# A planned attention and gate kernel: planning in forward and backward rounds, and another order of the first loads

## The chip, the cores and the metric

The kernel runs on one core of a Trainium2 chip. The metric is the device time in microseconds (us), as the median of several executions; one execution of each kernel is also taken with the hardware profiler. A core has five engines that run on their own and meet at semaphores: TensorE (PE, matrix products and transposes; its weight loads are shown apart as PEld), VectorE (DVE), ScalarE (ACT), GpSimd (POOL) and SyncE (SP). Loads and stores are DMAs, which SP, ACT and POOL issue. Here POOL's loads can also turn fp32 in memory into fp16 on the way.

## What is computed

Inputs are q, k, v of 8 batches x 8 heads x 576 positions x 64 columns, 32 packed queries p for each head, and three matrices. All are fp32, and so is the output of 8 x 576 x 512.

```python
def sm_attn(qq, kk, vv):
    a = softmax(qq @ kk.T / 8)
    return a @ vv
packed = sm_attn(p, k, v)               # 32 rows for each head
x = sm_attn(q, packed, packed)          # heads side by side: 576 x 512 a batch
proj = x @ w_proj                       # 512 -> 3 * 512
x1, x2, x3 = thirds of proj
x2_conv = irfft(rfft(x2, axis=seq) * rfft(filter, axis=seq))
out = (x1 * x2_conv * x3) @ w_out
```

The Fourier transforms are real ones along the 576 positions; here they are matrix products with cosine and sine tables.

## The kernel before

**Stages.** Each batch goes through four generators. `front(b)` (line 536) turns the keys on TensorE (`k_turn`), makes scores with the packed queries (`score1`, and `e1` by Exp), multiplies with the values (`pv`), turns the queries (`q_turn`, tile `qT`), and makes the second attention's weights (`score2` to `e2`; `normal` on DVE and POOL gives `a2n` and the tail). `turn(b)` (692) projects the 32 packed rows of each head with `w_proj` (`project`, tile `qm`), and takes the spectrum of the attention weights (`fp`, `fa`) and their transpose (`a2t`). So the attention's output is never formed: its product with each matrix is taken through the packed rows. `middle(b)` (754) makes the products with the spectrum of x2 (`f`, DVE's products with the filter `tt`, POOL's sums `gm`) and the two gates (`x1`, `x3`, kept as `w`). `back(b)` (809) does the inverse transform (products of `gm` and the table `ac`), multiplies with `w` to `y`, projects with `w_out` (`o`) and stores. `prologue_filter` (501) does the filter's spectrum once, in two fp16 halves (`fh`, `fl`, products into `hp`, results in `h3` and `htail`).

**Staggering.** `together` (883) interleaves the generators by the costs that they yield. In round b of the loop at line 911, `front(b)`, `turn(b-1)`, `middle(b-2)` and `back(b-3)` run together, with exceptions at the start.

**The planner.** Nothing is issued at once: a `Recorder` (line 145) keeps each instruction as an `Op`. `depend` (180) finds what must come before what, `plan` (205) plays the program with a price for each operation (`Op.ns`, `product`, `transfer_ns`) and the limits on buffers, and `emit` (369) issues in that order, each engine's order fixed. All instructions thus carry line 373 in the profile, and are told apart by tile names. The rule that orders ready operations on an engine is one line, `choose` (292): the first in the order in which the program recorded them. A load from POOL needs one of eight lanes, free again when it lands. Where PE has nothing ready, `filler` (266) puts in a product on zeros (`spin`), between 4.5 and 34 us of the plan and while a window of 3.4 us has less than 3.5 us of work.

**First loads.** From line 475 on: SP loads `ident`, the filter (six DMAs) and `ac`; ACT loads the tables `wc` (four) and `wt`; POOL loads p and q's tail of batch 0 (`load_small`), keys, values and queries of batch 0, three parts of `w_proj`, then batch 1 and `w_out`. `load(b)` for later batches is called two rounds ahead; from batch 4 on, SP turns the queries by a transposing DMA.

Of the kernel before, what the change touches and what calls it, by code (L numbers as in the profile page):

```python
# [17 lines left out]
P = 128  # L18
# [65 lines left out]
class Op:  # L84


    def __init__(self, n, engine, call, what, args, kw):
        self.n, self.engine, self.call, self.what, self.args, self.kw = n, engine, call, what, args, kw
        named = dict(kw)
        rest = [a for a in args if isinstance(a, bass.AP)]  # L90
        self.out = named.pop("out") if "out" in named else rest.pop(0)
        self.ins = rest + [a for a in named.values() if isinstance(a, bass.AP)]
        self.writes = [r for r in map(region, [self.out]) if r]
        self.reads = [r for r in map(region, self.ins) if r]
        size = lambda x: x.size() // x.shape[0]
        self.columns = size(self.out) if engine == "PE" else max(map(size, [self.out] + self.ins[:1]))
        self.need, self.then, self.unit = 0, [], None
        self.mode, self.place = (128, 128), None
        if engine == "PE":

            k, m = self.ins[0].shape[0], self.out.shape[0]
            self.mode = (64 if k <= 64 else 128), (m + 31) // 32 * 32
            self.place = self.reads[0][1] // self.mode[0], self.writes[0][1] // self.mode[1]

    def ns(self):
# [14 lines left out]
    def transfer_ns(self):  # L120
# [4 lines left out]
        if self.what == "dma_start_transpose":  # L125
            piece, size, self.piece_ns = 256, self.out.size() * 2, 22
        return size / piece * self.piece_ns / 16


# [12 lines left out]
class Recorder:  # L142
# [37 lines left out]
    def depend(self):  # L180

        seen, self.users, bank = {}, {}, {}
        for op in self.ops:
# [13 lines left out]
            if op.engine == "PE":  # L197

                before |= {bank[t] for t, *_ in op.writes if t in bank}
                bank.update({t: op for t, *_ in op.writes})  # L200
            op.need = len(before)
            for o in before:
                o.then.append(op)

    def plan(self):

        self.depend()
        opened = set()
        limit = {tag: bufs for kinds in self.slot.values() for tag, bufs in kinds}
# [56 lines left out]
        def filler(t):  # L266

            if 4500 < t < self.keep_warm and busy.get(int(t // window), 0) < warm + 300 and used["ps"] < limit["ps"]:
                op = self.spin()
# [7 lines left out]
        def fits(op, held):  # L277
# [7 lines left out]
            if any(used[tag] + held.get(tag, 0) + n > limit[tag] for tag, n in more.items()):  # L285
# [3 lines left out]
                return False  # L289
            return op.what[:9] != "dma_start" or op.engine != "POOL" or lanes[0] > 0  # L290

        def choose(e):
            held = {}
            return next((o for o in sorted(ready[e], key=lambda o: o.n) if fits(o, held)), None)

        def release(op, same):
            for o in op.then:
                if (o.engine == op.engine and op.what[:9] != "dma_start") == same:
                    o.need -= 1
# [3 lines left out]
        def issue(e, t):  # L303
            while free[e] <= t + 1e-6:
# [16 lines left out]
                order.append(op)  # L321
                if op.what[:9] == "dma_start":
                    took = 760 if e == "POOL" else 60
# [16 lines left out]
        while events:  # L340
            t, _, what, x = heapq.heappop(events)
            if what == "done":
                release(x, False)
# [22 lines left out]
        assert sum(op.n < 10 ** 9 for op in order) == len(self.ops), "the plan stops short"  # L366
        return order

# [11 lines left out]
def kernel(  # L380
# [56 lines left out]
    qTms = [const.tile([P, 2, 2, P], FP16, tag=f"qTm{r}", name=f"qTm{r}") for r in range(2)]  # L437
    filt = [sb([P, DM], FP32, tag="os", name=f"filt{i}", bufs=5) for i in range(5)]

# [7 lines left out]
    def load_small(b, n):  # L447

        pn = const.tile([P, n, 2, D], FP16, tag=f"pn{b}", name=f"pn_b{b}")
        qt = const.tile([P, n, H // 2, D], FP16, tag=f"qt{b}", name=f"qt_b{b}")  # L450
        nc.gpsimd.dma_start(pn[:], pflat[:, b:b + n, :, :])
        tail = q[b:b + n, :, 512:576, :].rearrange("b (g u) s d -> u s b g d", u=2)
        for u in range(2):
            nc.gpsimd.dma_start(qt[u * 64:(u + 1) * 64, :, :, :], tail[u])
        for x in range(n):
            small[b + x] = pn[:, x, :, :], qt[:, x, :, :]

    def load(b):
# [4 lines left out]
        qn = sb([P, H, 4 * D], FP16, tag="qn", name=f"qn_b{b}")  # L463
        nc.gpsimd.dma_start(kn[:], k[b].rearrange("h (p i) d -> p h (i d)", i=KI))
        nc.gpsimd.dma_start(vn[:], v[b].rearrange("h (p i) d -> p h (i d)", i=KI))
        nc.gpsimd.dma_start(qn[:], q[b, :, 0:512, :].rearrange("h (p i) d -> p h (i d)", i=4))
        if b in (2, 4):
# [8 lines left out]
    nc.sync.dma_start(ident[:], d_id.ap()[:])  # L476
    for i in range(4):
        nc.scalar.dma_start(wc[:, i, :], d_wc.ap()[:, i, :])
        nc.sync.dma_start(filt[i][:], fsrc[:, TILE_I[i], :])
    nc.scalar.dma_start(wt[:], d_wt.ap()[:])  # L480
    nc.sync.dma_start(filt[4][0:32, :], ftail[0])
    nc.sync.dma_start(filt[4][32:64, :], ftail[1])
    load(0)
    wsrc = moe_w_proj.rearrange("(g r) c -> r g c", r=P)
    for c in (1, 0, 2):
        nc.gpsimd.dma_start(wp[:, :, ts(c, DM)], wsrc[:, :, ts(c, DM)])
    nc.sync.dma_start(ac[:], d_ac.ap()[:])
    load(1)
# [410 lines left out]
    h = prologue_filter()  # L899
    some(h, 3)  # L900
    together((h, 4000.0), (front(0), 5500.0))
    first = turn(0)
# [27 lines left out]

    nc.spin, nc.keep_warm = spin, 34000
    nc.emit()

# [29 lines left out]
```

## Time and profile before

| | us |
|---|---|
| median of 4 runs | 204.92 |
| lowest, highest | 203.04, 207.04 |
| the profiled execution's own time | 206.22 |
| its span, first to last instruction | 204.4 |

| engine | busy us | share of the span |
|---|---|---|
| PE | 189.1 | 93% |
| DVE | 142.4 | 70% |
| POOL | 133.4 | 65% |
| ACT | 125.8 | 62% |

Names with a buffer number stand without it (`kn_b` is the keys of any batch). A line of the chain of waits is a start, a duration and what ran or was waited for; a group or a load names output<-input, the engine, the operation, and the count. "To landing" is from the issue to the completion of a DMA. PE's busy time counts a product from issue to its last result, and products overlap, so it isn't its use of the array.

### The profile page before, as it was taken

To read this page: it belongs to the slowest core of one execution; us is meant where nothing else is said; L and a number is where in the kernel's file an instruction comes from. 1 tells how busy PE (TensorE), PEld (TensorE's weight loads), DVE (VectorE), ACT (ScalarE), POOL (GpSimd) and SP (SyncE) were. 2 spreads that over 40 slices of the span, in tenths; PEclk is the share of its full clock that TensorE was granted. 3 is DMA by queue.
4 is the path that set the end of the run, shared out by engine and by line. 5 is a ranking of instruction groups with operands and counts; after the bars stand their busy time and mean duration, and the time that the engine had idled before them with its cause. 6 is when DMAs were issued, how large, how long until landed. Compare 5 with 4: busy or idle time off the path is not lost.

```text
span 204.4 us, 5828 instructions
## 1 busy us (share of the span) xinstructions
PE 189.1 (93%) x2419; PEld 117.3 (57%) x2419; DVE 142.4 (70%) x268; ACT 125.8 (62%) x265; POOL 133.4 (65%) x108
## 2 busy tenths in 40 slices
PE   3989978999999998999899999999999999999990
PEld 2335755665765674765476656656665565664640
DVE  4331683999528789876868589768876897688610
ACT  3234575775688968658766777676767746415140
POOL 7712339839753979986986796489548993972200
PEclk9997699999999999999999999999999999999997
DMA  6999999999999999999999993124012202413335
GB/s 162 268 245 201 207 196 201 204 201 189 201 185 260 207 152 161 140 146 196 257 230 166 168 197 110 50 81 128 3 51 84 76 0 104 129 29 115 95 115 141
DMA packets 44843, 30.96 MB, mean 151 GB/s; under 512 B 16336, under 2 KB 39376, under 8 KB 44816
## 3 DMA queue, kind: packets, MB, share of 16 engines
q0 software_dynamic: 29312, 16.52, 59.8%
q1 hardware_dynamic: 14784, 13.34, 26.8%
q10 hardware_dynamic: 720, 0.72, 1.3%
q8 instruction: 19, 0.31, 0.6%
q14 instruction: 8, 0.07, 0.1%
HBM read 35.55 MB, written 9.44 MB: 220 GB/s over the span
## 4 chain that ended last, share of the span: by engine, by line
PE 68%; POOL 10%; DMA 10%; ACT 5%; issue 2%; DVE 1%; POOLq 0%; ACTq 0%; DVEq 0%
PE x_b L373 24%; PE o_b L373 13%; PE f_b L373 6%; DMA kn_b<-in_k_dram 6%; PE fp_b L373 5%; PE s_b L373 4%; DMA qT_b<-qn_b 4%; POOL gm_b L373 3%; PE pv_b L373 3%; PE kTp_b L373 3%; POOL fa_b L373 2%; POOL tt_b L373 2%; ACT qm_b L373 2%; PE qp_b L373 2%; PE qTp_b L373 2%
## 5 line engine op out<-in xcount | busy, mean ns | idle before, releaser
L373 POOL TENSOR_TENSOR gm_b<-tt_b,tt_b 128x512 f16<-128x512 f32 (+1 forms) x28 | 39.2, 1427 | 9.7 <-DVE tt_b L373 9.2
L373 PE MATMUL x_b<-a2t_b,qm_b 128*128 128x512 f16 (+1 forms) x256 | 40.9, 286 | 0.0
L373 DVE TENSOR_TENSOR tt_b<-f_b,h 128x1024 f32<-128x1024 f32 x32 | 39.1, 1220 | 2.1 <-POOL gm_b L373 0.9
L373 PE MATMUL x_b<-ac,gm_b 128*128 128x64 f16 (+3 forms) x312 | 35.9, 253 | 2.0 <-POOL gm_b L373 1.7
L373 ACT ACTIVATE os_b<-o_b 128x512 f32<-128x512 f32 x36 | 21.6, 599 | 22.5 <-PE o_b L373 22.1
L373 PE MATMUL o_b<-wout,y_b 128*128 128x512 f16 x128 | 33.0, 379 | 0.1
L373 ACT CAST qm_b<-qp_b 128x512 f16<-128x512 f32 x48 | 25.3, 606 | 11.4 <-PE qp_b L373 11.4
L373 POOL TENSOR_TENSOR tt_b<-tt_b,tt_b 128x1024 f32<-128x1024 f32 x12 | 28.3, 2361 | 5.5 <-DVE tt_b L373 5.5
L373 DVE TENSOR_TENSOR w_b<-x1s_b,x_b 128x512 f32<-128x512 f32 (+1 forms) x40 | 25.1, 628 | 8.4 <-ACT x1s_b L373 8.1
L373 ACT COPY x1s_b<-x_b 128x512 f32<-128x512 f32 (+1 forms) x40 | 22.0, 551 | 12.6 <-PE x_b L373 9.2
L373 PEld LDWEIGHTS <-gm_b 128*128 128x128 f16 x312 | 22.0, 98 | 12.0 <-POOL gm_b L373 5.3
L373 ACT ACTIVATE e_b<-s_b 96x384 f16<-96x384 f32 (+1 forms) x48 | 24.2, 531 | 3.0 <-PE s_b L373 2.8
L373 POOL TENSOR_TENSOR fa_b<-ez_b 128x512 f16<-128x512 f32 x14 | 17.6, 1276 | 10.7 <-ACT ez_b L373 10.6
L373 PE MATMUL f_b<-qm_b,fa_b 128*128 128x512 f16 x80 | 23.9, 379 | 0.0
L373 DVE SCALAR_TENSOR_TENSOR y_b<-w_b,x_b 128x512 f16<-128x512 f32 x32 | 20.7, 683 | 3.3 <-PE x_b L373 3.2
L373 POOL TENSOR_TENSOR a_b<-e_b,zr_b 128x1152 f16<-128x1152 f16 (+2 forms) x10 | 17.4, 1740 | 7.4 <-ACT qm_b L373 7.4
L373 PEld LDWEIGHTS <-a_b 128*128 128x128 f16 x240 | 16.1, 98 | 9.2 <-POOL a_b L373 1.7
L373 PEld LDWEIGHTS <-qm_b 128*128 128x128 f16 x256 | 15.6, 98 | 7.5 <-issue 0.2
L373 PEld LDWEIGHTS <-y_b 128*128 128x128 f16 x128 | 11.9, 98 | 11.7 <-DVE y_b L373 1.0
L373 PE MATMUL kTp_b<-ident,kn_b 96*128 96x96 f16 x192 | 13.2, 208 | 1.7 <-DMA kn_b<-in_k_dram 1.4
L373 PEld LDWEIGHTS <-kn_b 96*128 96x128 f16 x192 | 10.9, 99 | 4.3 <-DMA kn_b<-in_k_dram 1.9
L373 ACT COPY kT<-kTp_b 128x576 f16<-128x576 f16 x16 | 10.4, 649 | 4.8 <-PE kTp_b L373 4.8
(78 smaller groups left out, 284.3 us busy)
## 6 DMA issues: line engine op xcount, KB each, us to landing
out_dram<-os_b SPq DMA_DIRECT2D x24, 256.0 KB, 2.4
kn_b<-in_k_dram POOLq DMA_DIRECT2D x8, 576.0 KB, 12.4
vn_b<-in_v_dram POOLq DMA_DIRECT2D x8, 576.0 KB, 15.2
qn_b<-in_q_dram POOLq DMA_DIRECT2D x8, 512.0 KB, 14.7
out_dram<-os_b SPq DMA_DIRECT2D x16, 128.0 KB, 2.5
wp<-in_moe_w_proj_dram POOLq DMA_DIRECT2D x3, 512.0 KB, 20.7
filt<-in_moe_filter_fft_dram SPq DMA_DIRECT2D x4, 256.0 KB, 5.3
out_dram<-os_b SPq DMA_DIRECT2D x16, 64.0 KB, 1.8
```

The lines of the kernel that those rows point to most:

```text
L373: ins = op.call(*op.args, **op.kw).ins
```

## The change

The planner gets a backward pass, `latest`: it plays the program from its end, picks on each engine by how late the last plan had put an operation, and so gives each operation a latest start. `plan` now runs up to eight rounds. A round schedules forward (`schedule`, the old body of `plan`), keeps the order if it ends earliest so far by the planner's own clock, and sets each operation's `first` from the backward pass. `choose` sorts by `first` and then by the recorded order; in the first round `first` is the recorded order.

The first loads are put in another order. On SP: `ident`, p and q's tail of batch 0 as fp32 (into buffers of `tt0`, `tt1`, cast by ACT), the filter's tail. On POOL: keys of batch 0 in two halves, `wc` as one load, the filter's 512 main rows as two loads of two tiles each (in buffers of `w`), `wt`, values, queries, three parts of `w_proj`, `ac`, batch 1, `w_out`. ACT issues no load. Spins may be put in from the moment the zeros they multiply are written, rather than from 4.5 us. At the start the filter's and batch 0's steps are interleaved from the first step on.

```diff
--- before.py
+++ after.py
@@ -94,13 +94,25 @@
         self.reads = [r for r in map(region, self.ins) if r]
         size = lambda x: x.size() // x.shape[0]
         self.columns = size(self.out) if engine == "PE" else max(map(size, [self.out] + self.ins[:1]))
-        self.need, self.then, self.unit = 0, [], None
+        self.need, self.then, self.unit, self.first = 0, [], None, n
         self.mode, self.place = (128, 128), None
         if engine == "PE":
 
             k, m = self.ins[0].shape[0], self.out.shape[0]
             self.mode = (64 if k <= 64 else 128), (m + 31) // 32 * 32
             self.place = self.reads[0][1] // self.mode[0], self.writes[0][1] // self.mode[1]
+
+    def dma(self):
+        return self.what[:9] == "dma_start"
+
+    def rates(self):
+
+        if self.dma():
+            return 760 if self.engine == "POOL" else 60, 4000 + self.transfer_ns()
+        if self.engine == "PE":
+            n = max(self.columns / 2.4 + 2.5, 27) if self.mode == (128, 128) else 25
+            return n, n + 175
+        return self.ns(), self.ns() + 60
 
     def ns(self):
         n, e = self.columns, self.engine
@@ -125,6 +137,10 @@
         if self.what == "dma_start_transpose":
             piece, size, self.piece_ns = 256, self.out.size() * 2, 22
         return size / piece * self.piece_ns / 16
+
+
+class Tick:
+    n = -1
 
 
 def region(ap):
@@ -198,14 +214,62 @@
 
                 before |= {bank[t] for t, *_ in op.writes if t in bank}
                 bank.update({t: op for t, *_ in op.writes})
-            op.need = len(before)
+            op.need = op.needs = len(before)
             for o in before:
                 o.then.append(op)
 
+    def latest(self):
+
+        before, open_, avail = {o: [] for o in self.ops}, {}, dict.fromkeys(self.ops, 0.0)
+        for o in self.ops:
+            open_[o] = len(o.then)
+            for x in o.then:
+                before[x].append(o)
+        ready, free, start = {e: [] for e in self.BEGIN}, dict.fromkeys(self.BEGIN, 0.0), {}
+        events = [(0.0, o.n, o) for o in self.ops if open_[o] == 0]
+        heapq.heapify(events)
+        while events:
+            t = events[0][0]
+            while events and events[0][0] <= t:
+                o = heapq.heappop(events)[2]
+                if o.n >= 0:
+                    heapq.heappush(ready[o.engine], (-o.t, o.n, o))
+            for e, queue in ready.items():
+                while queue and free[e] <= t:
+                    o = heapq.heappop(queue)[2]
+                    hold, land = o.rates()
+                    start[o] = free[e] = t + hold
+                    heapq.heappush(events, (free[e], -1 - o.n, Tick))
+                    for x in before[o]:
+                        open_[x] -= 1
+                        hold, land = x.rates()
+                        lag = 0 if x.engine == e and not x.dma() else max(0, land - hold)
+                        avail[x] = max(avail[x], start[o] + lag)
+                        if open_[x] == 0:
+                            heapq.heappush(events, (avail[x], x.n, x))
+        end = max(start.values())
+        return {o: end - t for o, t in start.items()}
+
     def plan(self):
 
         self.depend()
-        opened = set()
+        best = None
+        for _ in range(8):
+            for o in self.ops:
+                o.need = o.needs
+            try:
+                end, order = self.schedule()
+            except AssertionError:
+                break
+            if best is None or end < best[0]:
+                best = end, order
+            for o, t in self.latest().items():
+                o.first = t
+        return best[1]
+
+    def schedule(self):
+
+        opened, issued = set(), set()
         limit = {tag: bufs for kinds in self.slot.values() for tag, bufs in kinds}
         used = dict.fromkeys(limit, 0)
         left = {t: len(u) for t, u in self.users.items()}
@@ -265,7 +329,7 @@
 
         def filler(t):
 
-            if 4500 < t < self.keep_warm and busy.get(int(t // window), 0) < warm + 300 and used["ps"] < limit["ps"]:
+            if self.still in issued and t < self.keep_warm and busy.get(int(t // window), 0) < warm + 300 and used["ps"] < limit["ps"]:
                 op = self.spin()
                 left[op.writes[0][0]] = 1
                 return op
@@ -287,15 +351,15 @@
                     for tag, n in more.items():
                         held[tag] = max(held.get(tag, 0), n)
                 return False
-            return op.what[:9] != "dma_start" or op.engine != "POOL" or lanes[0] > 0
+            return not op.dma() or op.engine != "POOL" or lanes[0] > 0
 
         def choose(e):
             held = {}
-            return next((o for o in sorted(ready[e], key=lambda o: o.n) if fits(o, held)), None)
+            return next((o for o in sorted(ready[e], key=lambda o: (o.first, o.n)) if fits(o, held)), None)
 
         def release(op, same):
             for o in op.then:
-                if (o.engine == op.engine and op.what[:9] != "dma_start") == same:
+                if (o.engine == op.engine and not op.dma()) == same:
                     o.need -= 1
                     if o.need == 0:
                         ready[o.engine].append(o)
@@ -319,7 +383,9 @@
                     rest.extend((op.unit or [op])[1:])
                 ready[e].remove(op)
                 order.append(op)
-                if op.what[:9] == "dma_start":
+                issued.add(op)
+                op.t = t
+                if op.dma():
                     took = 760 if e == "POOL" else 60
                     if e == "POOL":
                         lanes[0] -= 1
@@ -339,6 +405,7 @@
             at(t, "free", e)
         while events:
             t, _, what, x = heapq.heappop(events)
+            last = t
             if what == "done":
                 release(x, False)
                 for r in {r[0] for r in x.reads + x.writes}:
@@ -364,7 +431,7 @@
             for e in free:
                 issue(e, t)
         assert sum(op.n < 10 ** 9 for op in order) == len(self.ops), "the plan stops short"
-        return order
+        return last, order
 
     def emit(self):
         last = {}
@@ -435,7 +502,9 @@
 
     kTr = [const.tile([P, 6 * KP + 32], FP16, tag=f"kT{r}", name=f"kT{r}") for r in range(4)]
     qTms = [const.tile([P, 2, 2, P], FP16, tag=f"qTm{r}", name=f"qTm{r}") for r in range(2)]
-    filt = [sb([P, DM], FP32, tag="os", name=f"filt{i}", bufs=5) for i in range(5)]
+    rows = [sb([P, 2, DM], FP32, tag="w", name=f"filt{i}") for i in range(2)]
+    filt = [rows[TILE_I[i] // 2][:, TILE_I[i] % 2, :] for i in range(4)]
+    filt.append(sb([P, DM], FP32, tag="os", name="filt4", bufs=5)[:])
 
     pflat = p.rearrange("b h j d -> (b h j) d").rearrange("(b t r) d -> r b t d", t=2, r=P)
 
@@ -448,10 +517,19 @@
 
         pn = const.tile([P, n, 2, D], FP16, tag=f"pn{b}", name=f"pn_b{b}")
         qt = const.tile([P, n, H // 2, D], FP16, tag=f"qt{b}", name=f"qt_b{b}")
-        nc.gpsimd.dma_start(pn[:], pflat[:, b:b + n, :, :])
+        to, qto, start = pn, qt, nc.gpsimd.dma_start
+        if b == 0:
+
+            to = sb([P, n, 2, D], FP32, tag="tt0", name="p32")
+            qto = sb([P, n, H // 2, D], FP32, tag="tt1", name="q32")
+            start = nc.sync.dma_start
+        start(to[:], pflat[:, b:b + n, :, :])
         tail = q[b:b + n, :, 512:576, :].rearrange("b (g u) s d -> u s b g d", u=2)
         for u in range(2):
-            nc.gpsimd.dma_start(qt[u * 64:(u + 1) * 64, :, :, :], tail[u])
+            start(qto[u * 64:(u + 1) * 64, :, :, :], tail[u])
+        if b == 0:
+            nc.scalar.copy(out=pn[:], in_=to[:])
+            nc.scalar.copy(out=qt[:], in_=qto[:])
         for x in range(n):
             small[b + x] = pn[:, x, :, :], qt[:, x, :, :]
 
@@ -461,9 +539,10 @@
         kn = sb([KP, H, KI * D], FP16, tag="kn", name=f"kn_b{b}")
         vn = sb([KP, H, KI * D], FP16, tag="vn", name=f"vn_b{b}")
         qn = sb([P, H, 4 * D], FP16, tag="qn", name=f"qn_b{b}")
-        nc.gpsimd.dma_start(kn[:], k[b].rearrange("h (p i) d -> p h (i d)", i=KI))
-        nc.gpsimd.dma_start(vn[:], v[b].rearrange("h (p i) d -> p h (i d)", i=KI))
-        nc.gpsimd.dma_start(qn[:], q[b, :, 0:512, :].rearrange("h (p i) d -> p h (i d)", i=4))
+        if b > 0:
+            nc.gpsimd.dma_start(kn[:], k[b].rearrange("h (p i) d -> p h (i d)", i=KI))
+            nc.gpsimd.dma_start(vn[:], v[b].rearrange("h (p i) d -> p h (i d)", i=KI))
+            nc.gpsimd.dma_start(qn[:], q[b, :, 0:512, :].rearrange("h (p i) d -> p h (i d)", i=4))
         if b in (2, 4):
             load_small(b, b)
         qT = sb([P, H, 2, P], FP16, tag="qT", name=f"qT_b{b}")
@@ -474,17 +553,23 @@
     fsrc = moe_filter_fft[0:512, :].rearrange("(p i) c -> p i c", i=4)
     ftail = moe_filter_fft[512:576, :].rearrange("(p e) c -> e p c", e=2)
     nc.sync.dma_start(ident[:], d_id.ap()[:])
-    for i in range(4):
-        nc.scalar.dma_start(wc[:, i, :], d_wc.ap()[:, i, :])
-        nc.sync.dma_start(filt[i][:], fsrc[:, TILE_I[i], :])
-    nc.scalar.dma_start(wt[:], d_wt.ap()[:])
-    nc.sync.dma_start(filt[4][0:32, :], ftail[0])
-    nc.sync.dma_start(filt[4][32:64, :], ftail[1])
     load(0)
     wsrc = moe_w_proj.rearrange("(g r) c -> r g c", r=P)
-    for c in (1, 0, 2):
-        nc.gpsimd.dma_start(wp[:, :, ts(c, DM)], wsrc[:, :, ts(c, DM)])
-    nc.sync.dma_start(ac[:], d_ac.ap()[:])
+    for u in range(2):
+        nc.sync.dma_start(filt[4][32 * u:32 * u + 32, :], ftail[u])
+    for g in range(2):
+        hh = slice(4 * g, 4 * g + 4)
+        nc.gpsimd.dma_start(loaded[0][0][:, hh, :], k[0, hh, :, :].rearrange("h (p i) d -> p h (i d)", i=KI))
+    nc.gpsimd.dma_start(wc[:], d_wc.ap()[:])
+    for n in range(2):
+        nc.gpsimd.dma_start(rows[n][:], fsrc[:, 2 * n:2 * n + 2, :])
+    nc.gpsimd.dma_start(wt[:], d_wt.ap()[:])
+    nc.gpsimd.dma_start(loaded[0][1][:], v[0].rearrange("h (p i) d -> p h (i d)", i=KI))
+    nc.gpsimd.dma_start(loaded[0][2][:], q[0, :, 0:512, :].rearrange("h (p i) d -> p h (i d)", i=4))
+    nc.gpsimd.dma_start(wp[:, :, ts(1, DM)], wsrc[:, :, ts(1, DM)])
+    nc.gpsimd.dma_start(wp[:, :, ts(0, DM)], wsrc[:, :, ts(0, DM)])
+    nc.gpsimd.dma_start(wp[:, :, ts(2, DM)], wsrc[:, :, ts(2, DM)])
+    nc.gpsimd.dma_start(ac[:], d_ac.ap()[:])
     load(1)
     nc.gpsimd.dma_start(wout[:], moe_w_out.rearrange("(g r) c -> r g c", r=P))
 
@@ -897,8 +982,7 @@
 
 
     h = prologue_filter()
-    some(h, 3)
-    together((h, 4000.0), (front(0), 5500.0))
+    together((h, 7300.0), (front(0), 5500.0))
     first = turn(0)
     some(first, 3)
 
@@ -929,6 +1013,7 @@
         return op
 
     nc.spin, nc.keep_warm = spin, 34000
+    nc.still = next(o for o in nc.ops if o.what == "memset" and o.out.tensor.name == pks[2].tensor.name)
     nc.emit()
```

## The prediction

> **What bounds the kernel now.** I read the slices of the span first, for where TensorE is slow and where the loads run.
>
> ```profile
> PE   3989978999999998999899999999999999999990
> PEclk9997699999999999999999999999999999999997
> DMA  6999999999999999999999993124012202413335
> ```
>
> A slice is 5.1 us. Loads fill the DMA engines to slice 24 (123 us), PE looks full from slice 8 on, and the clock is low in slices 4 and 5. A busy PE isn't one at its peak, so I priced the matmuls by their columns. Three 128x512 products follow each other in 0.65 us, 0.216 us each, 0.42 ns a column. Over the groups of instructions: 426 products of 512 columns take 91.8 us; 64, 88 and 88 of 256, 288 and 224 take 26.1; 176 transposes of 128 columns 9.8 and 192 of 96 columns 8.2; 672 products of 64 columns, at about 0.029, 19.5; the packed qp and pv products and the one-column sums 10.9. Sum 166 us, against 199.2 us when the last product ends: 33 us in which PE waits, spins or runs at half clock. Then the stretches of time, for where they are:
>
> ```profile
> 0.00:10.00 10.00, 6.76 (x20) 2.93 (x21) 4.15 (x16) 3.14 (x4) 7.71 (x14) 1.00 0.89 214
> 10.00:20.00 10.00, 8.60 (x67) 4.07 (x66) 3.00 (x7) 3.79 (x8) 2.04 (x4) 0.88 1.30 225
> 20.00:30.00 10.00, 8.68 (x150) 6.42 (x148) 7.41 (x17) 6.48 (x14) 2.78 (x4) 0.78 1.33 202
> ...
> 60.00:80.00 20.00, 19.00 (x318) 12.49 (x314) 16.52 (x33) 16.52 (x39) 14.92 (x11) 1.00 1.31 197
> 80.00:100.00 20.00, 19.56 (x277) 12.16 (x271) 15.64 (x28) 13.82 (x30) 17.42 (x14) 1.00 1.31 177
> ```
>
> The columns are PE, PEld, DVE, ACT, POOL, clock, DMA, GB/s. Up to 34.6 us, where batch 0's transform starts (f_b), PE has streamed some 13.5 us worth of columns: 21 us lost. From 40 to 120 us it streams 69 of 80 us, from 120 to 190 us 65 of 70 (my sums per ten us by the same price): 11 and 5 lost. From 60 to 100 us POOL, DVE and ACT each stand at 14 to 17.5 of 20, so there PE is held by chains through three nearly full engines. The chain that ended last names the start:
>
> ```profile
> 3.38 12.41 DMA kn_b<-in_k_dram
> 15.84 0.94 PE kTp_b L373 x18
> ...
> 21.24 1.09 PE pv_b L373 x42
> 22.33 0.97 PE spin L373 x4
> 23.30 1.47 PE qTp_b L373 x16
> 24.79 1.01 ACT qT_b L373
> ...
> 30.72 0.47 POOL a_b L373
> ...
> 34.60 0.43 PE f_b L373 x2
> ```
>
> Start, duration, what: keys land at 15.8 us, queries (issued at 4.91, 16.2 to landing) at 21.1, and 13.5 us later f_b begins. The keys are late because of what is beside them:
>
> ```profile
> kn_b<-in_k_dram POOLq DMA_DIRECT2D x1, 576.0 KB, 12.4
> vn_b<-in_v_dram POOLq DMA_DIRECT2D x1, 576.0 KB, 14.3
> filt<-in_moe_filter_fft_dram SPq DMA_DIRECT2D x4, 256.0 KB, 5.3
> wc<-c_wc ACTq DMA_DIRECT2D x4, 96.0 KB, 3.6
> ```
>
> (KB are those written; keys, values, queries and projection are fp32 in memory and are cast on the way, so twice that is read.)
>
> **What the Trainium skill says.** "DMA: Bandwidth & Descriptors", section "Issuing engines are not separate DMA queues": transfers from SP, ACT and POOL share the same 16 engines, and several issuers only save issue time. The trace agrees: while SP and ACT load 2.5 MB, POOL's keys take 12.4 us; alone on the engines such a load follows the one ahead by 2.9 us. Its section "Anatomy of one DMA — SWDGE (gpsimd) path" puts some 2 us fixed on a load; the SP's 32 KB ident, 2.3 us to landing, fits. "TensorE: Matmul & The Clock Gate", section "What's actually happening": half clock until about 3.4 us of activity, and again after an idle window of 3.4 us. Here the clock is half from 17.5 to 24.3 us, after PE had waited for the keys, and 16 transposes took 1.5 us that take 0.9 at full clock.
>
> **The change, part by part.** *Loads.* Rate: between the landing of kn (15.8) and of qn of batch 1 (24.12 + 14.9 = 39.0) POOL's queue alone reads 9.1 MB, 390 GB/s. Until the queries, the change has 5.8 MB to read: keys 1.18, small loads and filter tail 0.35, wc 0.39, filter rows 1.05, wt 0.33, values 1.18, queries 1.05, and no ac (0.59), which goes behind wp. POOL issues from 1.26, a load per 0.8 us; with 2 us fixed the data start near 4. At 390 GB/s: keys 7.8 us, wc 8.8, rows 11.5, wt 12.3, values 15.3, queries 18.0. Upper bound: at some 335 GB/s, which the mixed start of the trace moved, queries land at 21.3, no gain. I take 19. Batch 1's keys have the same bytes ahead as before: 31 to 33.5, against 33.4.
>
> POOL gets five issues it did not have (wc, two rows, wt, ac) and one more for the keys' second half, and loses three small ones: 3 x 0.8 = 2.4 us, in a stretch where POOL is busy 2.0 of 10 and 2.8 of 10; without that cover it would cost 2.4 us. The ninth issue must wait for a landing, but eight issues last to 7.7 and the first keys land before. ACT loses five issues (2.2 us) and gets two casts, by its 128x128 and 128x256 rows 0.28 + 0.37; its table load can start at 0.8 instead of 3.0. SP gets p, two tails of q and keeps two of the filter: 0.3 us each, SP has nothing else then. The filter rows now share buffers with w, first used after 36 us: nothing.
>
> *Order at the start.* The scores of batch 0 (24 transposes, 24 products, about 2 us) run at 8 to 12 us while the filter lands; the filter's 34 products (7.3 us at full clock, 14.6 at half) fit between 11.5 and 19. The spins, which start as soon as their zeros are written instead of at 4.5 us of the plan, make full clock likelier there. Then values are consumed when they land, and PE, ACT and DVE stand free for the queries. From queries to f_b: transposes 1.0, ACT copy 1.0, products 0.4, exp 0.55, sum and reciprocal 0.95, POOL's a 1.04 + 1.42, fp 1.5, ez to f_b 0.7, gaps 0.6: 9.2 us instead of 13.5. What goes is the 2.2 us from landing to the transposes, 0.6 of half clock and the 0.83 us wout issue between two a's on POOL; the rest are spins and gaps. Six DVE steps on h (0.68 each) still lie beside it; I take 10.5. f_b then starts at 29.5 to 30, some 4.5 us earlier. What is late next is batch 1's keys, 1.5 us earlier at best, so PE has batch 0 alone at first. I keep 4 us of the 4.5.
>
> *Forward and backward rounds.* Order on each engine now goes by the latest start that a backward pass gives, best of up to eight rounds by the planner's own clock. It adds no instruction. Its prices of operations agree with the trace (POOL 128x1152: 2.17 against 2.13 us; 128x1024 fp32: 2.35 against 2.36), but it gives a load 4 us and its transfer, some 7, where the trace shows 12 to 16. What it can win is the gap between 40 to 120 us (14% lost) and 120 to 190 (7%): 11 - 5.7 = 5 us. What it can lose is bounded below by the worst ten us of the steady part, 8.0 of 10 streamed. I take a gain of 2.
>
> Sum: 206.22 - 4 - 2 = 200.2 for the profiled execution, which was 1.3 us above the median 204.92 of its runs (203.04 to 207.04); against that median 198.9.
>
> **The rivals.** (1) *Start gained and given back*, 204 us: the loads remain one stream at 390 GB/s, and batch 1's keys come as before; PE, with a single batch in hand, waits for POOL and DVE, or the rounds find no better plan than the old order. For: DMA is full to 123 us, and f_b's batch has its own chain of 1.22 and 2.36 us steps. Against: batch 0's back part alone is 6.7 us of products. (2) *The new order is worse on the chip*, 210: PE takes its instructions in order, and an order that the planner's clock likes stalls where durations differ. Place: 40 to 190 us. Price: PE streams 134 of 150 us there, 8.94 of 10; each 0.1 less costs 1.7 us, so from 8.7 the 4 us of the start are gone, and at 8.4, between the worst and the mean, the run is 9.2 - 4 = 5 us longer. For: loads priced at half; the keys of batch 2, landing at 44.4 and used at 46.9, have 2.5 us to spare. Against: the prices of compute agree. (3) *Both win fully*, 194: 6 us at the start and 5 later.
>
> **How the numbers follow.** Forecast 0.40 (196 to 201.5), rival 1 0.20, rival 2 0.24, rival 3 0.16. The measurement tells about 2%, 4.1 us, from no change. Under 200.8 lie most of the forecast (0.36), nearly all of rival 3 and a sliver of rival 1: 0.53; over 209.0 lies some two thirds of rival 2: 0.16; 0.31 between. The range goes from inside rival 3 to inside rival 2, 193.5 to 208.
>
> **What would show it.** Keys at 7 to 9 us, queries at 18 to 21, no half clock after 10 us, f_b at 29 to 31; the last product as much earlier as f_b or more. If f_b is early and the last product isn't, rival 1 or 2, told apart by PE between 40 and 190 us. If the queries land after 22, the one queue is slower than 335 GB/s and the step on loads is wrong.

## The result and the profile after

The changed kernel takes 203.55 us (median of 43 runs, 202.51 to 205.15), the kernel before 203.89 in the same comparison. The ratio is 1.001, with a 95% interval of 0.9995 to 1.0025: no difference. The forecast was 198.9. (Some executions, mostly of the kernel before and of the rounds alone below, are 2 us or more longer at a lower mean clock of TensorE; both profiles of the kernel before and that of the rounds alone are of such executions, and the ratios leave these out, the medians don't.) The profiled execution took 203.57 us.

The slices of the span of the changed kernel:

```profile
PE   2287899989999999999999999999999999999990
PEclk9999999999999999999999999999999999999999
DMA  5999999999999999979999999133013202513335
```

TensorE now has less to do in the first 10 us, not more: the filter's products are gone from there. The chain of work that ended last, up to batch 0's transform (start, duration, what):

```profile
2.57 0.62 SPq L440
3.18 0.04 issue
3.23 0.69 SPq L440
3.92 0.04 issue
3.96 5.63 DMA filt<-in_moe_filter_fft_dram
9.63 0.04 issue
9.67 0.63 ACT fh L440
...
11.93 0.50 PE s_b L440 x6
...
20.06 1.01 ACT qT_b L440
...
23.95 2.06 DVE fl L440 x2
...
26.76 1.93 PE hp L440 x8
...
33.78 1.29 PE f_b L440 x6
```

Two things stand in it that the forecast had put beside the path: SP's small loads at the start, and the filter's subtractions and products behind the queries. The waits in the first 12 us say the first again (who waited for whom, total, times, longest):

```profile
DVE fl L440 <- ACT fh L440: 5.9, 1, 5.9
PEld L440 <- ACT qt_b L440: 4.5, 1, 4.5
ACT qt_b L440 <- DMA q<-in_q_dram: 4.3, 1, 4.3
```

SP issues p, ident, q's two tails and the filter's two from 0.74 us, at 0.46 to 0.75 us each; q's second tail lands at 8.1 and the filter's at 9.6. ACT's cast of q's tail stands ahead of its further copies, with the cast of the filter's tail behind it; PE's turning of q's tail stands ahead of the keys in PE's order, and DVE's subtraction for the filter's tail (`fl`) ahead of its other work. So three engines stand. The keys landed at 6.1 and 7.9 us, and are turned from 9.91. In the timeline of PE:

```profile
8.65 0.39 PE L440 MATMUL qTtp_b<-ident,qt_b 128*128 128x128 f16 x2 [3.99 <-ACT qt_b L440]
8.84 1.27 PE L440 MATMUL spin<-pk 128*128 128x256 f16 x5
9.91 1.17 PE L440 MATMUL kTp_b<-ident,kn_b 96*128 96x96 f16 x12
```

The second is in POOL's order of loads. It isn't the written one:

```profile
1.28 1.51 POOL L440 DMA_DIRECT2D kn_b<-in_k_dram  x2 [0.84 <-POOLq L1032]
2.79 0.78 POOL L440 DMA_DIRECT2D vn_b<-in_v_dram  x1
3.56 0.91 POOL L440 DMA_DIRECT2D qn_b<-in_q_dram  x1
4.46 0.58 POOL L440 DMA_DIRECT2D filt<-in_moe_filter_fft_dram  x1
5.00 0.57 POOL L440 DMA_DIRECT2D wc<-c_wc  x1
5.54 0.56 POOL L440 DMA_DIRECT2D filt<-in_moe_filter_fft_dram  x1
```

The rounds sort loads by latest start like everything else, and put values and queries ahead of factors and filter. Queries land at 14.0 us (3.56 + 10.4), 7 us earlier than before, and the filter's products run from 21.6 to 31.7. f_b starts at 33.6 us, where before it was 34.4, and the last product ends at 196.5, where it was 199.1. The last products in the timelines of PE, before and after (start, duration):

```profile
198.11 1.03 PE L373 MATMUL o_b<-wout,yt_b 128*128 128x512 f16 x4
```

```profile
195.46 1.03 PE L440 MATMUL o_b<-wout,yt_b 128*128 128x512 f16 x4
```

The planner's own clock ends at 199.75 us for the kernel before and at 195.05 for the changed one. So in the plan the change gains 4.7 us. In the plan PE turns q's tail at 5.8 us; on the chip it does at 8.65, and that lag grows to 5.7 us by 26 us and is 5 to 6 us to the end.

### The profile page after: what moved, and what is told of

It reads as the page before. It is cut to its first block, busy times and chain, and to the rows that moved or that the text cites. A ratio compares the mean times of both kernels' runs of the same rounds, so it can differ in the third digit from the quotient of the medians.

```text
span 201.8 us, 5784 instructions
## 1 busy us (share of the span) xinstructions
PE 183.9 (91%) x2405; PEld 115.3 (57%) x2405; DVE 142.7 (71%) x268; ACT 127.0 (63%) x267; POOL 135.3 (67%) x111
## 4 chain that ended last, share of the span: by engine, by line
PE 75%; DVE 10%; POOL 4%; ACT 3%; DMA 3%; issue 2%; SPq 1%; ACTq 0%; DVEq 0%
PE x_b L440 28%; PE o_b L440 13%; PE f_b L440 7%; PE fp_b L440 5%; PE s_b L440 5%; PE kTp_b L440 3%; PE pv_b L440 3%; PE qp_b L440 3%; DMA filt<-in_moe_filter_fft_dram 3%; DVE zs_b L440 2%; PE hp L440 2%; DVE tt_b L440 2%; DVE fl L440 2%; PE qTp_b L440 2%; SPq L440 1%
## 5 line engine op out<-in xcount | busy, mean ns | idle before, releaser
L440 ACT CAST qm_b<-qp_b 128x512 f16<-128x512 f32 x48 | 26.7, 592 | 12.2 <-PE qp_b L440 12.1
L440 PE MATMUL o_b<-wout,y_b 128*128 128x512 f16 x128 | 33.8, 379 | 0.0
L440 POOL TENSOR_TENSOR a_b<-e_b,zr_b 128x1152 f16<-128x1152 f16 (+2 forms) x10 | 17.8, 1783 | 9.3 <-DVE zs_b L440 5.4
L440 PE MATMUL kTp_b<-ident,kn_b 96*128 96x96 f16 x192 | 14.2, 215 | 1.1 <-DVE tt_b L440 1.0
L440 PEld LDWEIGHTS <-kn_b 96*128 96x128 f16 x192 | 11.9, 103 | 4.7 <-issue 2.6
L440 ACT COPY ez_b<-fp_b 128x512 f32<-128x512 f32 x16 | 9.4, 588 | 3.9 <-PE fp_b L440 3.7
## 6 DMA issues: line engine op xcount, KB each, us to landing
vn_b<-in_v_dram POOLq DMA_DIRECT2D x8, 576.0 KB, 15.4
kn_b<-in_k_dram POOLq DMA_DIRECT2D x7, 576.0 KB, 13.3
filt<-in_moe_filter_fft_dram POOLq DMA_DIRECT2D x2, 512.0 KB, 11.5
```

Source lines behind the costliest of these rows:

```text
L440: ins = op.call(*op.args, **op.kw).ins
```

## The experiments

The **start theory**: the plan is better, but the chip's start slips, since SP's small loads come later than planned and PE, ACT and DVE wait for them in order. The **queue theory**: the order of the loads, with values and queries ahead of the filter, is what costs. A third: the rounds gain nothing on the chip. Each kernel ran beside the kernel before, whose medians were 204.02 (first four), 204.23 (next four) and 204.49 us (last four).

**The loads alone.** One forward round, so the old rule of order; new loads, spins and early steps.

```diff
-        for _ in range(8):
+        for _ in range(1):
```

> The new loads and spins with a single forward round, so with the old rule of order. Start theory (the plan is better, but the chip's start slips, because SP's small loads and the casts behind them come later than the planner has it, and PE and ACT stand in order behind them): 205 to 207 us, f_b at 33 to 35 us, keys turned only after 8 us. Queue theory (the loads on one queue are as good as before, only the values and queries moved ahead of the filter did harm): 201 to 203.5. Rival that neither part matters on the chip: 203 to 204.

Measured: 208.56 us, 1.026 of before (1.022 to 1.030). The loads make the kernel slower by themselves, past what was expected. f_b starts at 37.7. The timeline of PE in its first 13 us:

```profile
11.25 0.39 PE L440 MATMUL qTtp_b<-ident,qt_b 128*128 128x128 f16 x2 [6.08 <-ACT qt_b L440]
11.44 1.27 PE L440 MATMUL spin<-pk 128*128 128x256 f16 x5
12.50 1.17 PE L440 MATMUL kTp_b<-ident,kn_b 96*128 96x96 f16 x12
```

Here q's tail lands at 10.8 us, beside tables and filter on POOL where it was values and queries; PE stands 6 us, and the keys are turned at 12.5.

**The rounds alone.** The kernel before, with only the planner of the change (the filler keeps its 4.5 us).

```diff
+    def latest(self):
+    ...
-            return next((o for o in sorted(ready[e], key=lambda o: o.n) if fits(o, held)), None)
+            return next((o for o in sorted(ready[e], key=lambda o: (o.first, o.n)) if fits(o, held)), None)
```

> The loads and the early steps of before, with the forward and backward rounds alone. Start theory: the 4 us that the planner's clock gains arrive on the chip, since the start has no small fp32 loads in it: 199 to 201 us, f_b at 30 to 32. Steady theory (the rounds gain nothing after 40 us, and little before): 203 to 204, f_b at 32 to 34.

Measured: 0.9895 of before (0.982 to 0.997), some 2 us or half of the 4 that were expected, in single runs from 201.0 to 209.3 us; the sign is clear, the size less. The rounds do gain on the chip, which the third theory denied. The profile, of an execution of 204.88 us, has f_b at 33.9, but at half clock from 13.3 to 23.5 us (columns as in the stretches of the prediction, the clock third from the end), so it doesn't tell where f_b stands otherwise:

```profile
13.30:23.50 10.20, 10.19 (x69) 4.77 (x68) 3.94 (x8) 5.16 (x11) 4.55 (x6) 0.50 1.36 207
```

**The written order of the first loads**, in the changed kernel.

```diff
             for o, t in self.latest().items():
-                o.first = t
+                o.first = o.n - 1e6 if o.dma() and o.n < self.written else t
```

(`written` is the count of operations recorded up to the last of these loads.)

> The changed kernel, with the first loads held in the order in which they are written (keys, tables and filter, values, queries), where the rounds had moved values and queries ahead of the filter. Queue theory: filter products fill the wait before the queries, f_b at 29 to 31, 200 to 202 us. Start theory: the keys are still turned after 8 us behind q's tail, 202.5 to 204.

Measured: 207.03 us, 1.017 (1.0115 to 1.0226): both expectations missed, on the slow side. q's tail is turned at 11.23 and the keys at 12.49, as with the loads alone. So it can't tell yet whether the order or the wait is at fault. It does tell that with the loads held in place the rounds take only 1.5 us off the loads alone (208.56 to 207.03), at about the same wait of PE (6.4 and 6.1 us).

**SP priced as the trace shows it.** Only the planner's price of a DMA issue on SP.

```diff
-            return 760 if self.engine == "POOL" else 60, 4000 + self.transfer_ns()
+            return 760 if self.engine == "POOL" else 600, 4000 + self.transfer_ns()
...
-                    took = 760 if e == "POOL" else 60
+                    took = 760 if e == "POOL" else 600
```

> The changed kernel, with the planner's price of a DMA issue on SP raised from 60 ns to 600, what the trace shows; nothing else. Start theory: little by the price alone while q's tail is still put ahead of the keys, 202 to 204; better, 200 to 202, if the keys come first on PE. Queue theory: no change, 203 to 204.

Measured: 200.79 us, 0.990 (0.984 to 0.995). PE now takes the keys first, in its timeline:

```profile
6.20 1.14 PE L440 MATMUL kTp_b<-ident,kn_b 96*128 96x96 f16 x12 [0.20 <-DMA kn_b<-in_k_dram]
```

f_b starts at 30.8, 2.8 us earlier than in the changed kernel, and the run is 2.8 us shorter.

**The small casts behind the keys.** The dearer SP changes the whole plan. This run keeps prices, loads and rounds, and adds one rule to the planner, not to the program's waits: ACT's casts of q's tail and of the filter's tail come after PE has turned the keys.

```diff
+        keys = [o for o in self.ops if o.engine == "PE" and name(o.out) == "kTp_b0"]
+        for op in self.ops:
+            if op.engine == "ACT" and (name(op.out) == "qt_b0" or any(name(x) == "filt4" for x in op.ins)):
+                keys[-1].then.append(op)
+                op.need = op.needs = op.need + 1
```

> The changed kernel, with one rule more for the planner: ACT's casts of q's tail and of the filter's tail, and so PE's turning of q's tail, come after the keys of batch 0 have been turned. Loads, prices and rounds as they are; by the planner's own clock this plan is 1.9 us longer. Start theory: keys turned from 6 to 8 us, f_b at 30.5 to 32, 200.5 to 202 us. Rival (the gain of the dearer SP price came from another place of the plan, not from the keys): 203.5 to 205.5.

Measured: 200.09 us, 0.982 (0.978 to 0.986), although the planner's clock calls this plan 1.9 us longer. The two casts are moved together, so the waits for q's tail and for the filter's tail are not told apart. Two lines of its timeline of PE:

```profile
6.01 1.14 PE L446 MATMUL kTp_b<-ident,kn_b 96*128 96x96 f16 x12
...
30.15 0.60 PE L446 MATMUL f_b<-qm_b,fa_b 128*128 128x512 f16 x2
```

Keys at 6.0, f_b at 30.15 us, 3.5 us earlier than in the changed kernel; the time is 3.5 us less.

**Both: SP's price and the written order.**

> The SP price of 600 ns and the written order of the first loads together: keys, tables and filter, then values and queries. Queue theory: with the keys turned early, the filter's products fit ahead of the values, f_b at 29 to 30.5 and 199 to 200.5 us. Rival (the order of values and filter doesn't matter, or values late cost as much as the filter late): 201 to 203.

The edits are those of the run with SP's price and of the one with the written order. Measured: 206.29 us, 1.017 (1.010 to 1.023): both expectations missed, on the slow side. The first half of the keys is turned at 6.7 us, but the wait isn't gone, since q's tail lands late beside tables and filter, and the second half of the keys stands behind it. PE's timeline:

```profile
11.42 0.28 PE L440 MATMUL qTtp_b<-ident,qt_b 128*128 128x128 f16 x2 [3.00 <-ACT qt_b L440]
11.55 0.68 PE L440 MATMUL kTp_b<-ident,kn_b 96*128 96x96 f16 x12
```

The filter's products begin at 16.4, and the queries, landed by 19, are turned only at 24.1 between them; f_b starts at 35.8. The queue theory falls in the form it had. Against SP's price alone the written order costs 5.5 us, with values and queries behind the filter and with q's tail later; which of the two costs how much isn't separated.

**Half of the filter's products.** The filter's lower fp16 half is left out: 17 products and DVE's subtractions.

```diff
-            nc.vector.tensor_tensor(out=fl[0:n, i, :], in0=filt[i][0:n, :], in1=fh[0:n, i, :], op=ALU.subtract)
...
-            for s, src in enumerate((fh, fl)):
+            for s, src in enumerate((fh,)):
```

> The kernel with SP at 600 ns, and of the filter's spectrum only the upper fp16 half: 17 of its 34 products and DVE's five subtractions are left out. If the filter's products lie in the path to f_b, behind the queries: 3 to 4 us less, 197 to 198 us, f_b at 27 to 28. If they lie beside it: 200 to 201, f_b at 30 to 31.

Measured: 199.02 us (four runs, 197.88 to 200.02), 1.8 less than with SP's price alone, f_b at 29.1 instead of 30.8. Between the two expectations: the filter's work is at least partly in the path. The profiled execution took 199.86 us and ran at half clock from 11.0 to 17.8 us, that of SP's price from 11.0 to 14.4, so the work left out is worth rather more than those 1.7 us of f_b. 17 products are 3.7 us at 0.216.

**The kernel before once more**, for a second profile.

> The kernel before once more, for its profile with TensorE's clock less disturbed than in the first: 202 to 204 us, f_b at 32.5 to 34, last product 163 to 164 us after f_b as in the other kernels, if the rounds gain nothing after f_b.

Measured: 206.33 us, at half clock from 16.4 to 26.6 us, f_b at 35.4, last product at 199.2, 163.8 us after it. The first two expectations missed, for the reason given in the section on the result; the third holds.

**The loads alone, small casts behind the keys.** The rule of "The small casts behind the keys" with one forward round.

> The new loads and spins with a single forward round, as in the run of the loads alone (208.6 us), and the rule that the small casts come after the keys. Start theory: the 5 us that PE stood there for q's tail come back, 203 to 204.5 us, keys from 6 to 8 us: the loads by themselves then cost and gain nothing against the kernel before. Rival (the new loads are bad by their order too): 206 to 208.

Measured: 205.11 us (14 runs), 1.0055 (1.001 to 1.010), between the two expectations. Of the 208.56, 3.5 us come back, not all 5: PE takes the keys at 6.2, but still stands 2.0 us ahead of q's tail and 1.3 after it, since the last copy of the turned keys stands behind both casts on ACT. Its timeline of PE:

```profile
11.36 0.29 PE L446 MATMUL qTtp_b<-ident,qt_b 128*128 128x128 f16 x2 [2.00 <-ACT qt_b L446]
11.48 0.93 PE L446 MATMUL spin<-pk 128*128 128x256 f16 x7
13.69 0.50 PE L446 MATMUL s_b<-pk,kT 128*128 128x64 f16 x6 [1.28 <-ACT kT L446]
```

Its chain of work that ended last, in that stretch:

```profile
14.83 6.19 PE hp L446 x24
21.02 0.62 PE pv_b L446 x54
21.64 1.61 PE hp L446 x7
23.25 1.01 PE qTp_b L446 x16
```

Values landed at 16.1 and queries at 19.6 stand behind the filter's products in PE's order.

**q's tail on POOL**, cast on the way, for batch 0 alone; its two loads stand right behind the two of the keys, and ACT's cast is gone.

```diff
-        for u in range(2):
+        for u in range(2) if b > 0 else ():
             start(qto[u * 64:(u + 1) * 64, :, :, :], tail[u])
...
-            nc.scalar.copy(out=qt[:], in_=qto[:])
+            tails.append((qt, tail))
...
+    qt0, tail0 = tails[0]
+    for u in range(2):
+        nc.gpsimd.dma_start(qt0[u * 64:(u + 1) * 64, :, :, :], tail0[u])
```

> The changed kernel, with q's tail of batch 0 loaded by POOL right behind the keys and cast on the way, as before the change, instead of as fp32 on SP. Plan and prices otherwise as in the change. Start theory: the same gain by another way, keys turned from 6 to 8 us, 200 to 202. Rival (only the rule on order helped): 203 to 204.

Measured: 200.59 us, 0.978 (0.974 to 0.983). Keys from 6.3 us, f_b at 31.0. In POOL's order the rounds put these two loads behind values, queries, filter and `wc` (6.07 us), and PE turns q's tail only at 19.1; the filter's tail, with less ahead of it on SP, lands at 6.5 instead of 9.6. So the plan moves here too. But a price, a rule and another queue give nearly the same time, and what the three share is that PE takes the keys from 6.0 to 6.3 us: that makes the wait the cause, and not one plan that happened to be good.

**The tables ahead of the filter**, with the small casts behind the keys: the POOL loads held as keys, values, queries, wc, wt, filter, w_proj.

> With the small casts after the keys, the first loads held in this order: keys, values, queries, the tables wc and wt, then the filter's rows, then w_proj. The table wt landed at 23.3 us behind the first part of w_proj, and fp of batch 0 needs it at 26.5. If the landing of wt sets f_b: f_b at 28 to 29.5, 198 to 199.5 us. If the filter's products or the casts set it: 200 to 201.

Measured: 201.21 us, 0.982 (0.976 to 0.987), f_b at 30.3. The landing of wt does not set f_b: it landed at 16.7 us, and fp, split among the filter's products, still ended at 26.4. What sets f_b at 30 after the keys are in time is not separated further: the filter's products (17 to 30 us), batch 0's own chain, and the loads of w_proj all lie there.

**Spins from 4.5 us**, with the small casts behind the keys.

```diff
-            if self.still in issued and t < self.keep_warm and busy.get(int(t // window), 0) < warm + 300 and used["ps"] < limit["ps"]:
+            if self.still in issued and 4500 < t < self.keep_warm and busy.get(int(t // window), 0) < warm + 300 and used["ps"] < limit["ps"]:
```

> With the small casts after the keys, and the spins allowed from 4.5 us of the plan as before the change. If the early spins bring full clock early and that counts: 201 to 202, half clock until 14 us or more. If not: 199.8 to 200.5.

Measured: 199.93 us, 0.976 (0.969 to 0.983), f_b at 28.6. The early spins bring nothing here. This is the fastest of the full kernels, 2.4% ahead of the kernel before; against 200.09 it is no difference.

**What the runs say together.** The gap from f_b's start to the end of the last product hardly moves. Each row is the profiled execution of a kernel:

| kernel | f_b starts, us | last product ends, us | between | this execution, us | ratio to before |
|---|---|---|---|---|---|
| before (two profiles) | 34.4; 35.4 | 199.1; 199.2 | 164.7; 163.8 | 206.22; 206.33 | 1 |
| loads alone | 37.7 | 201.5 | 163.8 | 208.62 | 1.026 |
| loads alone, casts behind keys | 34.4 | 197.9 | 163.5 | 205.0 | 1.0055 |
| rounds alone | 33.9 | 197.8 | 163.9 | 204.88 | 0.9895 |
| the change | 33.6 | 196.5 | 162.9 | 203.57 | 1.001 |
| the change, casts behind keys | 30.2 | 193.0 | 162.8 | 200.09 | 0.982 |
| the change, q's tail on POOL | 31.0 | 193.7 | 162.7 | 200.48 | 0.978 |

By medians, the rounds on the new loads are worth 5.0 us with the wait for q's tail (208.56 to 203.55) and 5.0 without most of it (205.11 to 200.09). The wait is worth 3.5 us both ways (208.56 to 205.11, 203.55 to 200.09). The new loads have 1 us more against them (205.11 against a median of 204.2), in which the rest of the wait is contained. Then 5.0 gained, 4.5 lost: the measured nothing.

The two parts don't simply add, though. On the old loads the rounds gain some 2 us (0.9895), and on the new ones, held in their written order, 1.5. So most of the 5.0 comes where the rounds are free to move the first loads as well; part of that is again a shorter wait for q's tail, 4.0 us in the changed kernel against 6.1 with the loads alone.

## Why the prediction was wrong

**The step that failed** is the one on SP, in the part on the loads: "0.3 us each, SP has nothing else then". The issue was priced (it took 0.46 to 0.75) and the landing was not. The tails of q have 256-byte pieces; they took 4.6 and 5.5 us to land beside POOL's loads, and everything behind the cast of the second stood still: ACT for 4.3 us, PE for 4.0, and DVE, which waits for the cast of the filter's tail behind it, for 5.9. I had the casts' durations right (0.28 + 0.37; they took 0.30 and 0.40) and did not name what is queued behind them on the three engines. The runs with the casts moved and with the tail on POOL show the price, 3.5 and 3.0 us. With that wait gone the kernel takes 200.09 us, near the 198.9 forecast and inside its own range of 196 to 201.5. But that the totals meet is luck: the forecast had 4 us from the loads and 2 from the rounds. With the old rule of order and most of the wait gone the loads give none (1.0055, f_b at 34.4), and the rounds on them give 5.0.

**The loads.** The rate was right: with the loads in written order (the loads alone) queries land at 5.75 + 12.9 = 18.7 us, where I took 19; keys land at 6.1 and 7.9, where I had 7.8. (The 2.3 us that I set beside the fixed 2 us of a POOL load are of a load on SP; the landing of the keys is the better sign.) But the order was read off the diff, and the rounds change it, as they sort loads too. So queries came at 14 us and the filter's rows at 15.4 and 17.6 (4.46 + 10.9, 5.54 + 12.1), and the step that fitted the filter's products "between 11.5 and 19" fell: they ran from 21.6 to 31.7. It fell without the rounds too: in the loads alone with the casts moved, the products ran from 14.6 to 25.0, and the values and queries, landed at 16.1 and 19.6, were used only at 21.1 and 23.2, between them.

**From queries to f_b** I had 9.2 us as a chain and took 10.5. It took 19.6 in the changed kernel, and 16 with the keys in time (14.2 to 30.15), since the filter's products and its casts and subtractions on ACT and DVE are then in that stretch. Half of the filter's products gave back 1.7 us of f_b or more.

**What f_b is worth.** I kept 4 of 4.5 us, for fear that batch 1's keys come too late. Those landed at 29.3 us (14.22 + 15.1), 4 us earlier than before, and f_b's shift passes to the end, to within about 1 us (table above; the widest among the runs with rounds that stand in the mean below is the one with later spins, f_b at 28.6 and the last product at 192.5). Rival 1 is near in time (204) and wrong in its mechanism: nothing was given back after f_b; it was lost ahead of it.

**The rounds.** I gave them 2 us, all after 40 us. On the new loads they are worth 5.0, nearly all ahead of f_b (34.4 to 30.2 us at the same loads), and some 0.7 after, at most: 163.2 us between f_b and the last product as the mean of seven plans with rounds (the change, the rounds alone, SP's price, casts behind the keys, q's tail on POOL, tables first, later spins; the half filter is left aside, and the written orders, one of which ran at half clock once more after f_b and shows 167.7), 163.9 of four without (the two profiles of before, the loads alone with and without the rule). Single profiles of one kind differ by as much, so the 0.7 is not shown. On the old loads, and on the new ones in their written order, the rounds gain 2 and 1.5 us: that is the size I gave, by chance, since it does not come where I had it. What I had missed most is that they order the loads. The stretch from 40 to 190 us, of the kernel before (second profile) and of the changed one, as PE, PEld, DVE, ACT, POOL, clock, DMA, GB/s:

```profile
40.00:190.00 150.00, 147.52 (x2019) 93.23 (x2018) 118.47 (x211) 103.11 (x222) 112.34 (x78) 1.00 0.82 139
```

```profile
40.00:190.00 150.00, 147.38 (x2013) 93.66 (x2014) 118.47 (x213) 102.50 (x218) 114.24 (x81) 1.00 0.87 140
```

That the better fill late in the run can be had in the middle was the error there: PE is as full as before. Rival 2, a worse order after 40 us, did not come either.

**The clock.** I expected no half clock after 10 us; it lasted to 16.8. The row PEclk doesn't show it, but the products do: here seven spins take 1.64 us, and 0.93 at full clock in the lines of "The loads alone, small casts behind the keys".

```profile
15.32 1.64 PE L440 MATMUL spin<-pk 128*128 128x256 f16 x7
```

This first half clock did not decide: the run with the later spins was as fast.

## What to carry to other kernels

A planner that orders by its own clock is only as good as its prices. A gain of 4.7 us on its clock became none, with an issue of 0.46 to 0.75 us in it as 0.06 and a landing of 4.6 to 8.4 us as 4 us and the transfer. Correcting the price of the issue brought 3 us, and so did a plan that is longer by its clock but keeps late small loads off the engines' fronts. The corrected price alone is no cure: with the loads in their written order the same price left PE waiting 3.0 us for q's tail, and the kernel at 206.29 us. When a change moves a load to another queue, follow its landing to the first instruction that waits for it, and name all that stands behind that instruction in order; and look in the new order itself, not in the diff, for where a planned instruction has gone.

## What the hardware showed that was not expected

The landing of a small load on SP goes with what POOL loads beside it. Each tail of q has the same 64 KB in 256-byte pieces: from issue to landing, the second took 5.3 to 5.5 us where values and queries (cast on the way) follow the keys on POOL, and 8.2 to 8.4 where the tables and the filter's rows do (the loads alone, with and without the rule, and both written orders). The first took 4.5 to 4.9 in all of them, and p, as many bytes and issued first, 2.0. What in those loads makes the difference was not tested.

Half clock came back though PE hardly stood. In the first profile of the kernel before it lasted 6.8 us, in the loads alone with the casts moved 3.4, in the rounds alone and the second profile of before 10.2: lengths of one, two and three times 3.4 us. The first two:

```profile
17.50:24.30 6.80, 6.59 (x109) 4.61 (x105) 2.35 (x7) 3.81 (x8) 1.74 (x3) 0.50 1.31 205
```

```profile
13.30:16.70 3.40, 3.01 (x14) 1.51 (x15) 2.91 (x5) 3.17 (x7) 1.23 (x3) 0.51 1.36 201
```

The prediction sets the first beside the idle window of 3.4 us that it quotes. PE's longest wait ahead of it after the start was 1.4 us, and ahead of the second 2.0, so here the trace doesn't bear that out, and why the clock fell stays open.
